# Halving the last network's inputs token by token and turning them by transposing transfers over DRAM instead of on TensorE, from the third group on

## The chip, the cores and the metric

The kernel runs on one core of one Trainium2 chip. The metric is the device time of one execution in microseconds, given as the median of several runs. Engines are named as the profile names them: PE (TensorE matmuls) and PEld (its weight loads), ACT (ScalarE), DVE (VectorE), POOL (GpSimd) and SP (SyncE), which issues most of the DMA transfers, in the order of its queue.

## The reference

Three stages over 3072 tokens of width 384. First a gated linear attention: per batch (4), head (8) and channel (48) a complex decay, a running state of 48 x 48, and an output y = q S. Then a mixture of 8 experts with a noisy gate: each token goes to its two best experts, and the results are summed with the gate's weights. Then the network that the change touches:

```
x = sum of the token's two expert rows, weighted        # 3072 x 384
h = maximum(maximum(x @ w1, x @ w2), x @ w3)            # 3072 x 768
out = h @ w_out                                         # 3072 x 384
```

## The kernel before

All operands of the large products are split into two f16 halves, a high and a low one, and each product is made as three f16 products (high x high, high x low, low x high) summed in PSUM.

Attention, gate and experts run first, in an order worked out by a planner written into the kernel (class `Order`). Behind them comes the last network, in program order, with the instructions of each engine put into that engine's queue by a list scheduler of the framework: what is ready first goes first, and among ready instructions the earlier in the program. It is this last part alone that the change touches.

The 24 blocks of 128 tokens are processed in seven groups, numbered here from 0: groups 0 and 1 have 2 blocks (256 tokens), groups 2 to 6 have 4 (512 tokens). Each group passes through four functions:

- `combine(g)` (L1508): for each of the group's blocks POOL gathers the two expert rows of every token from DRAM (tile `yg`, L1515, four buffers for each of the two), ACT scales the first (`za`, L1519, two buffers), DVE adds the scaled second (`z`, L1521). The blocks have tokens on the partitions.
- `turn(g)` (L1525): PE transposes each 128 x 128 piece of `z` into PSUM (`tz`, L1532, one buffer), three strips `k` of 128 channels, with the blocks of the group side by side; ACT writes the high half `zh` (L1533) and DVE the low half `zl` (L1534). Channels are then on the partitions.
- `hidden(g)` (L1537): for each of six strips `f` of the hidden width, PE makes three products u1, u2, u3 (L1553, 9 matmuls each: per `k` the pairs high-high, high-low, low-high), each into a PSUM tile `u` of five buffers. ACT copies the first (`mx`, L1561), DVE takes the maximum with the second (L1565) and third (L1566), ACT writes the high half `th` (L1567) and DVE the low half `tl` (L1568). The three PSUM tiles of a strip come free by L1561, L1565 and L1566.
- `last(g)` (L1570): for each block 18 matmuls (L1579) into `o` (two PSUM buffers), an ACT copy (L1582, three buffers), and a write of 192 KB by SP (L1585).

They are interleaved so:

```
combine(1)
for g in range(NG):
    hidden(g, range(0 if g else NPRE, KU), g + 1 if g + 1 < NG else None)
    last(g)
```

Within `hidden(g)` the next group is prepared. `turn(g + 1)` is issued behind the last matmul of the fifth strip (`f == KU - 2`), so its transposes stand on PE between matmuls near the end of `hidden(g)`. `combine(g + 1)`, for g of 1 to 5, is issued behind the first strip's ACT copy, so its ACT instructions stand behind that copy. Group 0 is gathered and turned earlier, by the planner.

The experts' part uses a transposing transfer already: `load_rows` (L1004) issues `dma_start_transpose` on SP, which reads 384 or 432 rows of 128 f16 values from the DRAM tensor `xs_rows` and puts them into `xa` with channels on the partitions. There are 96 of these.

Of the kernel before, what the change touches and what calls it, by code (L numbers as in the profile page):

```python
# [10 lines left out]
F16 = mybir.dt.float16  # L11
I32 = mybir.dt.int32
U32 = mybir.dt.uint32
AF = mybir.ActivationFunctionType
OP = mybir.AluOpType
# [17 lines left out]
    bufs=dict(bk=5, vg=2, wst=4, w1=1, w2=1, xa=2, hh=1, ya=2, ar=1, ai=1, iv=2, tn=1, r=1, ri=1, cs=3, fa=3,  # L33
           lam0=2, lam=6, lx=2, q=2, k=2, v=4, qr=3, kr=1, qc=2, kc=2, qt=2, kt=2, pm=2, xt=1, xhl=8, zp=1, fr=1,
           fh=4, car=1, sc=1, py=1, ps=1, lr=1, rw=3, w1b=1, w2b=1, raw=2, ua=1, vh=4, ch=1, cl=1),
# [213 lines left out]
def tile_kernel(ctx, tc, q, k, v, a_re, a_im, w_gate, w_noise, noise, w1, w2,  # L249
                u1, u2, u3, w_out, out):  # L250
    nc = tc.nc
    B, H, S, D = q.shape
    T = 128
    NC = S // T
    NI = B * NC
    NT = B * S
    HD = H * D
# [5 lines left out]
    KD = HD // 128  # L263
# [11 lines left out]

    FIRST = RA
    yf = nc.dram_tensor("yf_rows", (E * FIRST, HD), F32).ap()

    const = ctx.enter_context(tc.tile_pool(name="const", bufs=1, side="left"))
    EN = dict(POOL=nc.gpsimd, DVE=nc.vector)  # L280
# [80 lines left out]
    zl = const.tile([128, NI, 2 * E], F32, name="zl")  # L361
# [979 lines left out]
    GT = 512  # L1341
    GS = [2, 2] + [GT // T] * ((NT - GT) // GT)
# [4 lines left out]
    Z, TH = {}, {}  # L1347
# [65 lines left out]
    i = 0  # L1413
# [93 lines left out]
    def combine(g):  # L1507
        z = []  # L1508
        for t in range(GS[g]):
            i = sum(GS[:g]) + t  # L1510
            yy = []
            for s in range(2):
                y = fp.tile([128, HD], F32, name=f"yg{s}", bufs=4)
                src, row = (yf, sf) if (i + 1) * T <= FIRST else (ys, sy)
                nc.gpsimd.indirect_dma_start(out=y, out_offset=None, in_=src,  # L1515
                                             in_offset=bass.IndirectOffsetOnAxis(ap=row[:, i, s:s + 1], axis=0))
                yy.append(y)
            a = fp.tile([128, HD], F32, name="za", bufs=2)
            nc.scalar.activation(a, yy[0], AF.Copy, scale=wt[:, i, 0:1])  # L1519
            zt = fp.tile([128, HD], F32, name="z", bufs=TG + 1)  # L1520
            nc.vector.scalar_tensor_tensor(zt, yy[1], wt[:, i, 1:2], a, op0=OP.mult, op1=OP.add)  # L1521
            z.append(zt)
        Z[g] = z

    def turn(g):  # L1525
        z = Z[g]
        n = GS[g] * T
        zh, zl_ = (fp.tile([128, KD, GT], F16, name=x) for x in ("zh", "zl"))
        for k in range(KD):
            p = ptz.tile([128, GT], F32, name="tz")  # L1530
            for t in range(GS[g]):
                nc.tensor.transpose(p[:, t * T:(t + 1) * T], z[t][:, k * 128:(k + 1) * 128], ident)  # L1532
            nc.scalar.activation(zh[:, k, :n], p[:, :n], AF.Copy)  # L1533
            nc.vector.tensor_tensor(zl_[:, k, :n], p[:, :n], zh[:, k, :n], op=OP.subtract)  # L1534
        Z[g] = zh, zl_

    def hidden(g, fs_, then=None):  # L1537
# [6 lines left out]
        for f in fs_:  # L1544
            fs = slice(f * 128, (f + 1) * 128)
            ps = []
            for nm in ("u1", "u2", "u3"):
                uh, ul = U[nm]
                p = pu.tile([128, GT], F32, name="u")
                m = 0  # L1550
                for k in range(KD):
                    for w, x in ((uh, zh), (uh, zl_), (ul, zh)):
                        ins = nc.tensor.matmul(p[:, :n], w[:, k, fs], x[:, k, :n], start=(m == 0),  # L1553
                                               stop=(m == 3 * KD - 1))
                        m += 1
                ps.append(p[:, :n])
            if f == KU - 2 and then is not None:
                with tc.issue_after(ins.ins):
                    turn(then)
            a = fp.tile([128, GT], F32, name="mx", bufs=3)[:, :n]  # L1560
            ins = nc.scalar.activation(a, ps[0], AF.Copy)  # L1561
            if not f and 0 < g < NG - 1:
                with tc.issue_after(ins.ins):
                    combine(g + 1)
            nc.vector.tensor_tensor(a, a, ps[1], op=OP.max)  # L1565
            nc.vector.tensor_tensor(a, a, ps[2], op=OP.max)  # L1566
            nc.scalar.activation(th[:, f, :n], a, AF.Copy)  # L1567
            nc.vector.tensor_tensor(tl[:, f, :n], a, th[:, f, :n], op=OP.subtract)  # L1568
# [18 lines left out]
    fp = ctx.enter_context(tc.tile_pool(name="f", bufs=2, side="left"))  # L1587
# [3 lines left out]
    beyond()  # L1591
    po = ctx.enter_context(tc.tile_pool(name="po", bufs=2, space=PSUM))
# [3 lines that stand above are left out]
# [32 lines left out]
```

## Time and profile before

| | |
|---|---|
| median of 3 runs | 977.07 us (976.3 to 977.68) |
| the profiled execution | 977.96 us, span of its instructions 975.9 us |
| PE busy | 928.4 us (95% of the span) |
| DVE, ACT, POOL busy | 597.2 us (61%), 482.3 us (49%), 144.0 us (15%) |
| the last network's part | from about 677 us to the end |
| of the chain that ended last | PE 72%, DVE 11%, DMA 6%, ACT 6% |

The page of the profile gives busy times by engine, the same in 40 slices of the span (24.4 us each), and the chain of work that ended last: followed back from the last instruction, at each step to what released it or to the instruction before it on its engine. An engine's idle time costs something only where that chain passes through it. A line of the chain or of the timeline that merges several instructions gives their count behind an x.

### The profile page before, as it was taken

What the parts mean: (1) busy time and instruction counts of PE and PEld (TensorE: products, weight loads), DVE (VectorE), ACT (ScalarE), POOL (GpSimd) and SP (SyncE); (2) the same over time, 40 slices, a digit from 0 to 9 for tenths busy, and PEclk for the clock granted to TensorE, in tenths of its full rate; (3) what the DMA queues carried; (4) which work ended last, traced back from release to release, by engine and by line L of the source; (5) the groups of instructions that cost most, each with busy time, mean ns of one, the idle gap of its engine ahead of it and who ended that gap; (6) DMA issues with size and microseconds to landing.
All of it is one profiled execution on the core that took longest, in us unless ns stands there. A gap on an engine that the chain in (4) does not pass through costs nothing.

```text
span 975.9 us, 17033 instructions
## 1 busy us (share of the span) xinstructions
PE 928.4 (95%) x6372; PEld 587.5 (60%) x6372; DVE 597.2 (61%) x1407; ACT 482.3 (49%) x930; POOL 144.0 (15%) x201
## 2 busy tenths in 40 slices
PE   3989898999999999997989999998999999999998
PEld 1868787876666667653545555554784545454544
DVE  5988889996556658668988774542343232324231
ACT  7999889977444646523354444331232222322221
POOL 0102375231010004300010000000433030300000
PEclk9999998999999999998999999999999999999999
DMA  9999996995666565697658786631322020200000
GB/s 151 201 216 274 189 228 166 186 219 161 173 191 179 170 201 150 205 297 210 193 175 243 218 217 163 189 114 45 89 82 74 25 73 25 74 25 9 25 9 33
DMA packets 228636, 143.09 MB, mean 147 GB/s; under 512 B 179784, under 2 KB 216264, under 8 KB 228552
## 3 DMA queue, kind: packets, MB, share of 16 engines
q1 hardware_dynamic: 222408, 123.11, 49.3%
q0 software_dynamic: 6144, 18.88, 6.5%
q8 instruction: 50, 0.82, 0.4%
q14 instruction: 34, 0.28, 0.1%
HBM read 89.78 MB, written 41.88 MB: 135 GB/s over the span
## 4 chain that ended last, share of the span: by engine, by line
PE 72%; DVE 11%; DMA 6%; ACT 6%; issue 3%; SPq 1%; POOL 0%; ACTq 0%; POOLq 0%; DVEq 0%
PE u L1553 21%; PE bk L1035 8%; PE bk L1055 8%; PE o L1579 7%; PE bk L1096 7%; PE bk L1122 6%; PE sc L730 3%; DMA wst<-in_moe_w_dram 2%; PE bk L719 2%; PE ps L769 2%; PE py L748 2%; DMA raw<-in_moe_w_dram 1%; PE bk L552 1%; PE py L751 1%; PE bk L633 1%
## 5 line engine op out<-in xcount | busy, mean ns | idle before, releaser
L1055 PE MATMUL bk<-w,hh 128*128 128x384 f16 x576 | 99.2, 332 | 7.0 <-DVE w L985 5.8
L435 ACT ACTIVATE hh<-bk 128x384 f16<-128x384 f32 (+1 forms) x128 | 64.3, 508 | 79.7 <-PE bk L1096 42.4
L1035 PE MATMUL bk<-xa,w 128*128 128x384 f16 x576 | 99.0, 326 | 0.6 <-DMA xa<-xs_rows 0.6
L983 ACT ACTIVATE w<-wst 128x768 f16<-128x768 f32 (+1 forms) x77 | 71.4, 933 | 55.6 <-DMA wst<-in_moe_w_dram 24.0
L985 DVE SCALAR_TENSOR_TENSOR w<-wst,w 128x768 f16<-128x768 f32 (+1 forms) x77 | 81.0, 1066 | 11.7 <-ACT w L983 11.0
L1055 PEld LDWEIGHTS <-hh 128*128 128x128 f16 x576 | 56.6, 99 | 46.0 <-issue 10.1
L1122 PEld LDWEIGHTS <-hh 128*128 128x128 f16 x576 | 55.0, 98 | 39.8 <-issue 4.6
L1035 PEld LDWEIGHTS <-w 128*128 128x128 f16 x576 | 55.4, 98 | 36.1 <-issue 2.4
L1567 ACT ACTIVATE th<-mx 128x512 f16<-128x512 f32 (+1 forms) x42 | 23.8, 568 | 107.2 <-DVE mx L1566 107.2
L441 DVE COPY ya<-bk 128x384 f32<-128x384 f32 x30 | 16.7, 557 | 76.5 <-PE bk L1055 45.5
L938 POOL DMA_INDIRECT xs_rows<-xhl,sl x48 | 58.9, 1227 | 31.0 <-issue 10.1
L1565 DVE TENSOR_TENSOR mx<-mx,u 128x512 f32<-128x512 f32 (+1 forms) x42 | 25.6, 609 | 59.2 <-PE u L1553 59.1
L1515 POOL DMA_INDIRECT yg<-ys_rows,sy x42 | 42.8, 1020 | 120.7 <-ACT za L1519 105.1
L730 PE MATMUL sc<-qt,kt 96*128 96x128 f32 x384 | 53.5, 283 | 2.2 <-DVE pm L734 0.7
L1096 PE MATMUL bk<-xa,w1b 128*128 128x432 f16 x288 | 53.4, 346 | 1.8 <-DVE hh L1105 1.8
L1096 PE MATMUL bk<-xa,w 128*128 128x432 f16 x288 | 53.2, 346 | 0.0
L730 PEld LDWEIGHTS sc<-qt,kt 96*128 96x128 f32 x384 | 48.2, 194 | 6.4 <-issue 1.9
L1105 DVE SCALAR_TENSOR_TENSOR hh<-bk,hh 128x432 f16<-128x432 f32 x64 | 37.8, 603 | 17.0 <-ACT hh L435 16.8
L1122 PE MATMUL bk<-w2b,hh 128*128 128x384 f16 x288 | 48.2, 326 | 0.0
L1122 PE MATMUL bk<-w,hh 128*128 128x384 f16 x288 | 48.2, 326 | 0.0
L1521 DVE SCALAR_TENSOR_TENSOR z<-yg,wt,za 128x384 f32<-128x384 f32 x22 | 12.7, 614 | 56.6 <-ACT za L1519 52.0
L1579 PE MATMUL o<-woh,th 128*128 128x384 f16 x144 | 46.9, 326 | 0.0
(243 smaller groups left out, 2032.6 us busy)
## 6 DMA issues: line engine op xcount, KB each, us to landing
wst<-in_moe_w_dram SPq DMA_DIRECT2D x45, 512.0 KB
wst<-in_moe_w_dram SPq DMA_DIRECT2D x60, 384.0 KB
xs_rows<-wst SPq DMA_DIRECT2D x8, 1152.0 KB
ys_rows<-ya SPq DMA_DIRECT2D x48, 192.0 KB
raw<-in_moe_w_dram SPq DMA_DIRECT2D x9, 768.0 KB
ar<-in_a_re_dram SPq DMA_DIRECT2D x24, 192.0 KB
ai<-in_a_im_dram SPq DMA_DIRECT2D x24, 192.0 KB
q<-in_q_dram SPq DMA_DIRECT2D x24, 192.0 KB
```

The lines of the kernel that those rows point to most:

```text
L435: nc.scalar.activation(o, i, f, **kw)
L730: nc.tensor.matmul(tl("sc", (i, g))[:, j, :], tl("kt", i)[:, h, :], tl("qt", i)[:, h, :], start=True, stop=True)
L938: ins = nc.gpsimd.indirect_dma_start(out=xs, out_offset=bass.IndirectOffsetOnAxis(ap=sl[:, i, t:t + 1], axis=0), in_=tl("xhl", i), in_offs ...
L983: nc.scalar.activation(hi, src, AF.Copy, scale=scale)
L985: nc.vector.scalar_tensor_tensor(lo, src, scale, hi, op0=OP.mult, op1=OP.subtract)
L1035: nc.tensor.matmul(tl(*b)[:, :RA], tl("w1", e)[:, w, k, f * 128:(f + 1) * 128], tl("xa", e)[:, x + k, :RA], start=(k == m == 0), stop=(k = ...
L1055: nc.tensor.matmul(tl(*b)[:, :HD], tl("hh", e)[:, a, f, t * 128:(t + 1) * 128], tl("w2", e)[:, w, f], start=(f == m == 0), stop=(f == KF - ...
L1096: nc.tensor.matmul(tl(*b)[:, :RB], tl(n1, inst)[:, w, k, f * 128:(f + 1) * 128], tl("xa", xi)[:, x + k], start=(k == m == 0), stop=(k == K ...
L1122: nc.tensor.matmul(tl(*b)[:, :HD], tl("hh", xi)[:, a, f, ts_], tl(n2, inst)[:, w, f], start=(f == m == 0), stop=(f == KF - 1 and m == 2))
L1515: nc.gpsimd.indirect_dma_start(out=y, out_offset=None, in_=src, in_offset=bass.IndirectOffsetOnAxis(ap=row[:, i, s:s + 1], axis=0))
L1553: ins = nc.tensor.matmul(p[:, :n], w[:, k, fs], x[:, k, :n], start=(m == 0), stop=(m == 3 * KD - 1))
L1579: nc.tensor.matmul(p, a[:, f, ts_], w[:, f], start=(m == 0), stop=(m == 3 * KU - 1))
```

## The change

From group 2 on, `combine` does the halving, and `turn` returns at once. For each block, ACT copies `z` to f16 as the high half and DVE subtracts it to make the low half, both into one tile `zr` (128 tokens x 2 x 384 f16, three buffers), and SP writes the tile to a new DRAM tensor `z_rows`. Once the group's blocks are written, six transposing transfers on SP read 512 rows x 128 columns each and fill the three strips of `zh` and then the three of `zl`. Groups 0 and 1 stay as they were.

```diff
+    zs = nc.dram_tensor("z_rows", (NT, 2 * HD), F16).ap()
...
             zt = fp.tile([128, HD], F32, name="z", bufs=TG + 1)
             nc.vector.scalar_tensor_tensor(zt, yy[1], wt[:, i, 1:2], a, op0=OP.mult, op1=OP.add)
             z.append(zt)
+            if g > 1:
+                zr = fp.tile([128, 2, HD], F16, name="zr", bufs=3)
+                nc.scalar.activation(zr[:, 0], zt, AF.Copy)
+                nc.vector.tensor_tensor(zr[:, 1], zt, zr[:, 0], op=OP.subtract)
+                nc.sync.dma_start(zs[i * T:(i + 1) * T].rearrange("t (z d) -> t z d", z=2), zr)
         Z[g] = z
+        if g > 1:
+            r, n = sum(GS[:g]) * T, GS[g] * T
+            Z[g] = tuple(fp.tile([128, KD, GT], F16, name=x) for x in ("zh", "zl"))
+            for j in range(2 * KD):
+                nc.sync.dma_start_transpose(Z[g][j // KD][:, j % KD, :n], zs[r:r + n, j * 128:(j + 1) * 128])
 
     def turn(g):
+        if g > 1:
+            return
         z = Z[g]
```

## Rows read from the trace of the kernel before

**Rows 1.** The page's second part: TensorE's granted clock in 40 slices, tenths of full.
```profile
PEclk9999998999999999998999999999999999999999
```

**Rows 2.** Stretches of groups 1 and 2: length, busy by engine (count), clock, DMA share, GB/s.
```profile
707.60:732.80 25.20, 25.20 (x211) 20.50 (x210) 11.33 (x25) 9.48 (x21) 7.96 (x8) 1.00 0.26 80
732.80:781.05 48.25, 48.25 (x248) 24.16 (x246) 16.31 (x25) 13.05 (x23) 8.26 (x8) 1.00 0.16 50
```

**Rows 3.** The chain in order of time, groups 1, 2 and 6: start, us, what.
```profile
707.56 14.74 PE u L1553 x135
722.30 0.44 PE tz L1532 x4
...
724.16 0.65 PE tz L1532 x4
...
732.83 29.14 PE u L1553 x135
761.97 0.44 PE tz L1532 x4
...
763.92 0.56 PE tz L1532 x4
...
769.35 11.70 PE o L1579 x72
...
925.70 34.97 PE u L1553 x162
```

**Rows 4.** Line L1532, all transposes: min/median/max ns, first and last start, shape.
```profile
L1532 PE MATMUL tz<-ident,z x66: 272/273/329, 697.6 to 910.9; 128*128 128x128 f32 x66
```

**Rows 5.** Groups by shape from 676 us on: busy us, mean ns; idle and releaser.
```profile
L1568 DVE TENSOR_TENSOR tl<-mx,th 128x512 f16<-128x512 f32 x30 | 20.7, 691 | 18.1 <-ACT th L1567 18.1
L1567 ACT ACTIVATE th<-mx 128x512 f16<-128x512 f32 x30 | 18.9, 628 | 90.2 <-DVE mx L1566 90.2
L1534 DVE TENSOR_TENSOR zl<-tz,zh 128x512 f16<-128x512 f32 x15 | 10.4, 691 | 11.9 <-ACT zh L1533 11.8
L1533 ACT ACTIVATE zh<-tz 128x512 f16<-128x512 f32 x15 | 9.0, 597 | 26.4 <-PE tz L1532 26.4
L1568 DVE TENSOR_TENSOR tl<-mx,th 128x256 f16<-128x256 f32 x12 | 5.1, 423 | 4.3 <-ACT th L1567 4.3
```

**Rows 6.** Timeline of ACT, then DVE, around the combine of group 2.
```profile
708.92 1.11 ACT L1519 ACTIVATE za<-yg,wt 128x384 f32<-128x384 f32 x2
...
711.53 0.39 ACT L1561 ACTIVATE mx<-u 128x256 f32<-128x256 f32 x1 [0.17 <-PE u L1553]
...
710.96 1.14 DVE L1521 SCALAR_TENSOR_TENSOR z<-yg,wt,za 128x384 f32<-128x384 f32 x2
712.02 0.41 DVE L1566 TENSOR_TENSOR mx<-mx,u 128x256 f32<-128x256 f32 x1
```

**Rows 7.** Timeline of SP: transposing transfers of 384 rows, and groups 0 and 1's output writes.
```profile
196.66 1.13 SPq L1004 DMA_TRANSPOSE xa<-xs_rows  x1
...
215.81 6.30 SPq L1004 DMA_TRANSPOSE xa<-xs_rows  x5
...
705.19 28.53 SPq L1585 DMA_DIRECT2D out_dram<-o  x4
```

**Rows 8.** Timeline of PE: a matmul that waited for such a transfer.
```profile
201.86 0.97 PE L1035 MATMUL bk<-xa,w 128*128 128x384 f16 x5 [0.56 <-DMA xa<-xs_rows]
```

**Rows 9.** Stretches (columns as in rows 2): behind five transfers, after a stall, an output write.
```profile
222.00:223.00 1.00, 1.00 (x9) 0.61 (x7) 1.00 (x5) 1.00 (x4) 0.00 (x0) 1.00 0.43 98
223.00:224.00 1.00, 1.00 (x8) 0.61 (x7) 0.99 (x3) 0.96 (x4) 0.22 (x1) 1.00 0.00 0
683.50:686.70 3.20, 3.20 (x16) 2.27 (x17) 1.25 (x3) 0.42 (x1) 2.32 (x3) 0.50 0.23 66
706.00:707.00 1.00, 1.00 (x8) 0.61 (x7) 0.00 (x0) 0.00 (x0) 0.00 (x0) 1.00 0.53 197
```

**Rows 10.** Timeline of PE: the stall ahead of that stretch.
```profile
683.50 0.39 PE L1553 MATMUL u<-ua,u3l 128*128 128x256 f16 x1 [3.48 <-issue]
```

## The prediction

> **What bounds the kernel now.** The change touches the last network alone, so I first read which engine the end hangs on there. The chain in order of time [rows 3] shows, from 683 us to the last output block, nothing but PE pieces: products of the hidden layer (u), output products (o), and between them short pieces of transposes (tz). The stretches of groups 1 and 2 say the same from the other side: PE is busy for the whole length of each, 25.20 of 25.20 us and 48.25 of 48.25, while DVE is busy 16.31, ACT 13.05 and POOL 8.26 us of the 48.25 and the DMA engines 0.16 of it [rows 2]. The clock granted there is 1.00 of full, that is its upper level of 2.4 GHz [rows 1, 2]. So PE work taken out of these groups comes off the end, and work put on ACT, DVE and SP costs nothing while it is done before PE asks for its result or for the PSUM tiles that ACT and DVE drain.
>
> **What goes.** The transposes of groups 2 to 6, 60 of the 66 [rows 4]. One lasts 273 ns by itself, but they are pipelined, and what counts is their share of the chain. Group 2's stand in group 1's hidden part: 0.44 + 0.65 + 0.65 = 1.74 us. Group 3's stand in group 2's: 0.44 + 0.56 + 0.56 = 1.56 us; the pieces of 0.65 and 0.56 stand twice each, and groups 4 to 6 repeat group 3's pattern [rows 3]. Sum: 1.74 + 4 x 1.56 = 7.98 us. The waits for the single tz buffer lie inside these pieces. The check against a group that has no transposes in it: group 6's 162 hidden matmuls take 34.97 us, group 2's part lasts 769.35 - 732.83 = 36.52 us, a difference of 1.55 [rows 3]. I take 7.9 us, with 7.8 to 8.0 as its bounds.
>
> Per group ACT loses three `zh` copies (3 x 0.60) and DVE three `zl` subtractions (3 x 0.69) [rows 5].
>
> **What comes on ACT and DVE.** Per group four `zr` copies of 384 columns on ACT, each no more than the 0.63 us of a 512-column copy from SBUF, and four subtractions on DVE between 0.42 (256 columns) and 0.69 (512), so about 0.55 [rows 5]. That is 2.5 against 1.8 us before on ACT and 2.2 against 2.1 on DVE: the totals hardly move. What does move is their place: they now sit at the first strip of the hidden part, beside the work that frees PSUM tiles. Five `u` tiles rotate and a strip uses three, so a tile is asked for again five products later. In a group of 512 a product takes 9 x 29.14/135 = 1.94 us. The last combine of group 2 shows the tightest place, group 1 with 256 tokens, where a product takes 9 x 14.74/135 = 0.98 us [rows 3]: the tile that DVE frees at 712.43 (first strip's third product) is asked for at 707.56 + 7 x 0.98 = 714.4, and the tile that ACT frees at 711.92 (second strip's first) at 707.56 + 8 x 0.98 = 715.4 [rows 3, 6]. Margins: 2.0 and 3.5 us. If all four subtractions stand ahead of the first of these, 2.2 us are added and PE waits 0.2 us. There is also one new wait: `zr` has three buffers, so the fourth copy waits for the first write to land. In ACT's queue the rest of the strips' copies stand behind it. The first copy can start when the first `z` is there, two operations of some 0.6 us after 708.92 [rows 6], about 710.2, its subtraction ends near 711.4, and a write's bytes were all moved within 706 to 707 us after an issue at 705.19, 1.8 us [rows 7, 9]; so the fourth copy starts no later than about 713.9 with a little queueing, and a subtraction queued behind it ends by 715.2. The worst order would make PE wait some 1.5 us here, the best nothing. I take nothing, since DVE and ACT are filled by readiness and the maximum (L1566) already slips in as soon as its product is there. For groups of 512 the same margins are twice as long, 4 us and more, and cover it.
>
> **What comes on SP and the DMA engines.** Per group four writes of 192 KB and six transposing transfers. SP issues five transfers back to back in 6.30 us, 1.26 each, and a single one in 1.13 [rows 7]; the issue is what limits them, since in the last full microsecond of those five the DMA engines are busy 0.43 of the time at 98 GB/s, and from 223.00 on they move nothing, 0.9 us after the last issue ended at 222.11 [rows 9]. That 0.9 us is the lower bound of issue end to landing. The upper one is the matmul that waited for its transfer until 201.86: if it was the one issued at 196.66, 5.2 us from its start and 4.1 from its end [rows 7, 8]. The new transfers have 512 rows instead of 384; as no row shows them, I bound one by 1.13 to 1.68 us (1.26 x 512/384), and take 1.26, as the issue was what took the time.
>
> **When they are due.** Group 2 first. Its last `z` is ready at 712.10 [rows 6], the last `zr` between 713.4 and 715.5. The write takes 1.8 us, in the worst case as long as the slow transfer, 5.2. Six transfers last 6.8 to 10.1 us, and the last lands 0.9 to 4.1 us later. Earliest: 713.4 + 1.8 + 6.8 + 0.9 = 722.9. With the middle values 714.5 + 1.8 + 7.6 + 2.5 = 726.4. All four worst: 715.5 + 5.2 + 10.1 + 4.1 = 734.9. PE would come to group 2's hidden part at 732.83 - 1.74 = 731.1; its second matmul needs the fourth transfer, and the eighth, 1.5 us later, the sixth. So the sixth is due at 732.6: 6 us of margin in the middle, 2.3 us short in the worst corner. Beyond the margin a microsecond late costs a microsecond. For groups 3 to 6 the combine ends likewise some 7 us after the start of a hidden part of 36.5 us, with 11.70 us of output products behind it [rows 3]: at least 20 us of margin.
>
> Nothing else waits on SP in that time. Its four output writes of groups 0 and 1 stand between 705.19 and 733.72 [rows 7], two at the start and two at the end, and SP is otherwise idle there.
>
> **The sum.** The profiled execution took 977.96 us, span 975.9. Minus 7.9 that is 970.06. The median of the runs is 0.89 lower, 977.07, and gives 969.2 us, which I predict.
>
> **The rivals.** (a) A small price at group 1 and 2: the worst orders above, 0.2 to 1.5 us of PSUM waits and up to 2.3 us of late input, and slow matmuls behind a wait: after a stall of 3.48 us PE ran at a granted clock of 0.50, its lower level of 1.2 GHz, for 3.2 us and lost 1.6 us by it [rows 9, 10]. Together 0.5 to 5.4 us, time 969.7 to 974.6. For it: the margin of 2.0 us; against it: ready work goes first.
>
> (b) The transfers don't overlap each other, so that each takes the 5.2 us from issue to landing. Then six take 31.2 us. Groups 3 to 6 make it: group 3's could start some 10 us behind 732.83 and is due 48 us behind it. Group 2 doesn't: 714.5 + 1.8 + 31.2 = 747.5 against 732.6, 14.9 us late plus the 1.6 us of slow clock: 969.2 + 16.5 = 985.7, slower. It decides from about 3.8 us per transfer on (716.3 + 6 x 3.8 = 739.1, 6.5 late, which with the 1.6 eats the gain). Against it: five in 6.30 us with the engines empty 0.9 us later [rows 7, 9]. The Trainium skill, page "VectorE: DVE Perf Modes", section "The three transpose paths", speaks for it: it gives a 128x128 bf16 transpose 390 ns on TensorE and 1309 ns through the DMA crossbar, and its rules prefer TensorE when the result may go to PSUM. By that price, added up, a group's 24 pieces would take an estimated 31.4 us, and the time would be that of this rival; the trace disagrees, as five transfers of three pieces each were through in 7.2 us, 0.48 us a piece.
>
> (c) SP's queue is the new bound: the transfers of group g + 1 stand behind the output writes of group g, whose last is issued only after PE's last output product. Then each group's first two products wait about 1.0 + 6 x 1.26 + 0.9, some 9 us, and 1.6 us for the clock, five times: about 1020 us. Against it: the writes and transfers are earlier in the program and ready some 20 us earlier.
>
> (d) No gain: PE waits somewhere else for as much as it saves. The chain shows no second path within 8 us, so this is only a coincidence of (a) and (b).
>
> **Chances.** All hidden, 968.4 to 970.4: 0.70. (a): 0.14. (d): 0.05. (b): 0.06. (c) and other orders that starve PE: 0.05. What a measurement can tell from no change is 0.2%, 2 us: faster (below 975.1) 0.84, same 0.05, slower 0.11. The range takes in the forecast and (a), 967.8 to 974.6.
>
> **What would show it.** Right: no tz piece in the chain after 705 us but group 1's; hidden parts of 17.7 us (162 x 14.74/135) for group 1 and 35.0 for groups 2 to 5; PE without gaps; six transfers of 1.1 to 1.7 us on SP ending before 728 and then once per group. The forecast is wrong if PE's first matmul of a group waits for `zh` or `zl` (late input), or PE waits for `mx` at the second or third strip (PSUM), or if the transfers on SP stand behind the output writes.

## The result, and the profile after

The changed kernel took 968.5 us (median of 6 runs, 967.16 to 971.24), the one before 977.11 us beside it (6 runs): a ratio of 0.9908, 95% interval 0.9883 to 0.9932, so 6.6 to 11.4 us less. The forecast was 969.2 us, 7.9 us less, in a range of 967.8 to 974.6. Its profiled execution took 968.75 us, span 966.9.

The chain of waits of the kernel after, in order of time (start, us, what), answers to [rows 3]:
```profile
699.40 0.39 PE tz L1546 x2
...
706.62 17.68 PE u L1567 x162
724.31 5.85 PE o L1593 x36
730.16 34.96 PE u L1567 x162
765.12 11.70 PE o L1593 x72
776.82 34.97 PE u L1567 x162
...
963.57 0.49 ACT o L1596
```
The hidden part of group 2 was 29.14 us of matmuls, then three pieces of transposes between smaller ones; now it is one piece of 162 matmuls in 34.96 us, and group 1's is 17.68. No tz piece is left behind group 1's, at 700 us. The profile's list of waits has one line for PE behind 676 us, the stall at group 0 that stood there before as well [rows 10], and none for `zh`, `zl` or `mx`:
```profile
PE u L1567 <- issue: 3.5, 1, 3.5
```
From group 1's first matmul to the last copy of the output, the time was 972.45 - 707.56 = 264.89 us before and is 963.57 - 706.62 = 256.95 us after: 7.94 us less, against the 7.9 of the forecast.

The same stretches as in [rows 2], one group each (length, busy by engine, clock, DMA share, GB/s):
```profile
706.60:730.20 23.60, 23.60 (x200) 19.34 (x198) 11.29 (x26) 9.33 (x23) 8.64 (x8) 1.00 0.61 152
730.20:776.80 46.60, 46.60 (x235) 22.92 (x234) 16.31 (x26) 13.10 (x24) 8.44 (x8) 1.00 0.30 85
```
PE fills both from end to end. DVE (11.29 and 16.31 us, before 11.33 and 16.31) and ACT (9.33 and 13.10, before 9.48 and 13.05) are as busy as they were; what grew is the DMA share, 0.26 to 0.61 and 0.16 to 0.30. The clock stays at 1.00, its upper level of 2.4 GHz.

The new operations, grouped by shape (busy us, mean ns, idle before):
```profile
L1528 DVE TENSOR_TENSOR zr<-z,zr 128x384 f16<-128x384 f32 x20 | 10.8, 555 | 0.0
L1527 ACT ACTIVATE zr<-z 128x384 f16<-128x384 f32 x20 | 10.3, 515 | 4.4 <-DVE z L1523 3.5 <-DMA z_rows<-zr 0.9
```

### The profile page after: what moved, and what is told of

Read it like the earlier page. It is cut to its first block, busy times and chain, and to the rows that moved or that the text cites. A ratio compares the mean times of both kernels' runs of the same rounds, so it can differ in the third digit from the quotient of the medians.

```text
span 966.9 us, 17029 instructions
## 1 busy us (share of the span) xinstructions
PE 920.8 (95%) x6312; PEld 582.0 (60%) x6312; DVE 596.9 (62%) x1412; ACT 482.6 (50%) x935; POOL 144.4 (15%) x201
## 4 chain that ended last, share of the span: by engine, by line
PE 75%; DVE 11%; ACT 5%; DMA 4%; issue 3%; POOL 0%; SPq 0%; ACTq 0%; POOLq 0%; DVEq 0%
PE u L1567 22%; PE bk L1098 8%; PE bk L1037 8%; PE bk L1057 8%; PE bk L1124 7%; PE o L1593 7%; PE sc L732 3%; PE bk L721 2%; PE ps L771 2%; PE py L750 2%; PE bk L554 1%; PE bk L1131 1%; DMA wst<-in_moe_w_dram 1%; PE bk L635 1%; PE py L753 1%
## 5 line engine op out<-in xcount | busy, mean ns | idle before, releaser
L1579 DVE TENSOR_TENSOR mx<-mx,u 128x512 f32<-128x512 f32 (+1 forms) x42 | 25.6, 610 | 61.9 <-PE u L1567 61.8
L940 POOL DMA_INDIRECT xs_rows<-xhl,sl x48 | 58.2, 1212 | 31.4 <-issue 9.2
L1580 DVE TENSOR_TENSOR mx<-mx,u 128x512 f32<-128x512 f32 (+1 forms) x42 | 25.6, 610 | 36.0 <-PE u L1567 35.6
```

The lines of the kernel that those rows point to most:

```text
L940: ins = nc.gpsimd.indirect_dma_start(out=xs, out_offset=bass.IndirectOffsetOnAxis(ap=sl[:, i, t:t + 1], axis=0), in_=tl("xhl", i), in_offs ...
```

## The experiments

The chip that ran the first four was slower for every kernel: the kernel before took 1008.23 us there (21 runs). So they are compared by ratio, and by the trace from a group's first matmul on, where PE kept the same pace on both chips (162 hidden matmuls in 34.96 us).

**Both ways of turning at once.**
```diff
-            Z[g] = tuple(fp.tile([128, KD, GT], F16, name=x) for x in ("zh", "zl"))
+            X = tuple(fp.tile([128, KD, GT], F16, name=x, bufs=1) for x in ("xh", "xl"))
             for j in range(2 * KD):
-                nc.sync.dma_start_transpose(Z[g][j // KD][:, j % KD, :n], zs[r:r + n, j * 128:(j + 1) * 128])
+                nc.sync.dma_start_transpose(X[j // KD][:, j % KD, :n], zs[r:r + n, j * 128:(j + 1) * 128])
...
 def turn(g):
-        if g > 1:
-            return
```


> TensorE's transposes stay as before, and the whole added work runs beside them: the copies and subtractions to zr, the writes, and the six transposing transfers of each group, into two spare tiles that nobody reads. Theory 1 (the gain is the 60 transposes taken off TensorE, 7.9 us, and all that was added is covered): same as before, 977 +- 1 us, tz pieces of 1.5 to 1.7 us per group in the chain. Theory 2 (the added work costs TensorE something and the removal is worth more than 7.9): 1 us or more slower than before. Theory 3 (part of the gain, about 1 us, comes from a shift ahead of the last network): 976 us or less.

1008.3 us, ratio 0.9985 (0.9957 to 1.0013): no difference. Its chain has the tz pieces of [rows 3] again:
```profile
762.58 29.14 PE u L1565 x135
791.72 0.44 PE tz L1544 x4
...
793.67 0.56 PE tz L1544 x4
...
1002.21 0.49 ACT o L1594
```
From group 2's first matmul to the last copy it is 1002.21 - 762.58 = 239.63 us, in the kernel before 972.45 - 732.83 = 239.62. All that the change adds costs nothing there, with the transposes still on PE. Ahead of it, group 1 took 762.58 - 736.67 = 25.91 us in this trace, in the kernel before 25.27. Of the 0.64 us more, 0.5 are a wait of PE's transposes for a `zl` subtraction on DVE, and DVE had stood idle until 749.63, 5 us after its last `zr` operation. What held it up the trace doesn't show; the doubled transfers below have the same copies and subtractions in group 1 and no such delay (23.7 us, without transposes).

**Neither way.**
```diff
 def combine(g):
-            if g > 1:
-                zr = fp.tile([128, 2, HD], F16, name="zr", bufs=3)
...
-                nc.sync.dma_start(zs[i * T:(i + 1) * T].rearrange("t (z d) -> t z d", z=2), zr)
-        if g > 1:
...
-                nc.sync.dma_start_transpose(Z[g][j // KD][:, j % KD, :n], zs[r:r + n, j * 128:(j + 1) * 128])
+        if g == 2:
+            Z["x"] = tuple(fp.tile([128, KD, GT], F16, name=x, bufs=1) for x in ("xh", "xl"))
+            for x in Z["x"]:
+                nc.gpsimd.memset(x, 0.5)
 def turn(g):
         if g > 1:
+            Z[g] = Z["x"]
             return
```


> Neither way of turning: no transposes on TensorE from group 2 on, no halving to zr, no write, no transposing transfer; groups 2 to 6 read two constant tiles instead of their inputs, so their output is not the reference's. This is the floor of what the change can give. Theory 1: equal to the changed kernel, 968.5 to 969.2 us. Theory 2: 1 us or more below the changed kernel, 967 us or less. Theory 3: as theory 1 from the hidden part on, with TensorE reaching group 1 as early as in the changed kernel.

1001.23 us, ratio 0.9937 (0.9913 to 0.9961), its interval overlapping that of the changed kernel.
```profile
759.94 34.96 PE u L1562 x162
...
993.35 0.49 ACT o L1591
```
From group 2 on 993.35 - 759.94 = 233.41 us; the changed kernel has 963.57 - 730.16 = 233.41. There the changed kernel stands on the floor. Ahead of that, group 1, this kernel can't tell: on this chip PE lost 1.0 us in two waits for nothing that the profile shows, which the traces of the kernels before and after don't have.

**Each transfer twice.** Before each useful transposing transfer one into a spare tile.
```diff
+            X = tuple(fp.tile([128, KD, GT], F16, name=x, bufs=1) for x in ("xh", "xl"))
             for j in range(2 * KD):
+                nc.sync.dma_start_transpose(X[j // KD][:, j % KD, :n], zs[r:r + n, j * 128:(j + 1) * 128])
                 nc.sync.dma_start_transpose(Z[g][j // KD][:, j % KD, :n], zs[r:r + n, j * 128:(j + 1) * 128])
```


> Each transposing transfer is preceded by an equal one into a spare tile, 12 per group. By the margins of theory 1: SP begins the twelve of group 2 at about 718.6 us, at 1.26 us each the eighth is issued by 728.7 and the twelfth by 733.7, and lands 1 to 2 us later; TensorE wants group 2 at 730.2 and the last half 1.5 us later. So group 2 is 3 to 4 us late, with up to 1.6 us more for the lower clock behind the wait; groups 3 to 6 keep more than 10 us of margin: 971.5 to 974.5 us, one wait of TensorE in the whole tail. Rival (the transfers are limited by the DMA engines, not by their issue): longer than 1.3 us each, group 2 later by 10 us and more, 979 us or more. Rival (more margin than worked out): no change, 968.5 us.

1004.82 us, ratio 0.9973 (0.995 to 0.9997), 3.6 us above the kernel with neither by the medians. SP's timeline around group 2, and PE's two waits there:
```profile
753.09 1.26 SPq L1537 DMA_TRANSPOSE zh<-z_rows  x1
...
764.29 1.26 SPq L1537 DMA_TRANSPOSE zl<-z_rows  x1
765.59 1.26 SPq L1536 DMA_TRANSPOSE xl<-z_rows  x1
766.89 1.26 SPq L1537 DMA_TRANSPOSE zl<-z_rows  x1
```
```profile
767.03 0.38 PE L1569 MATMUL u<-zl,u1h 128*128 128x512 f16 x1 [1.75 <-DMA zl<-z_rows]
...
767.47 0.38 PE L1569 MATMUL u<-zh,u1h 128*128 128x512 f16 x1
769.71 0.59 PE L1569 MATMUL u<-zl,u1h 128*128 128x512 f16 x1 [1.86 <-DMA zl<-z_rows]
```
Twice as many transfers still follow each other at 1.26 us, so the rival with longer ones falls. The doubling alone doesn't tell whether the issue or the DMA engines set that pace; that 384 rows took the same 1.26 us [rows 7], with the DMA engines 0.43 busy [rows 9], speaks for the issue. PE now waits for the last `zl` strips, twice, 3.6 us in all, and only at group 2: the groups behind it follow each other in 46.66 us as in the changed kernel. The price is more than the waits: from group 1's first matmul to the last copy it is 1003.11 - 740.45 = 262.66 us, 5.71 more than in the changed kernel and inside the 3 to 6 expected, as PE ran at a lower granted clock behind the second wait (0.75 over these 5 us):
```profile
770.00:775.00 5.00, 5.00 (x19) 2.06 (x18) 2.53 (x5) 3.55 (x7) 2.21 (x3) 0.75 0.21 65
```
The trace also measures the landing: the last transfer's issue ends at 768.15, PE goes on at 769.71, 1.6 us later.

**The transfers behind the output writes.** The six transfers move into a function `fetch`, issued on SP behind the last output write of the group before.
```diff
 def last(g):
-            nc.sync.dma_start(out[r:r + T], o)
+            W = nc.sync.dma_start(out[r:r + T], o)
+        with tc.issue_after(W.ins):
+            fetch(g + 1)
```


> The six transposing transfers of each group are issued on SP behind the last output write of the group before, in place of some 20 us earlier: the cover is taken away, five times. Theory 1: each group's first products wait for four transfers and their landing, about 5 to 7 us behind the last output write's issue, which itself is about 1 us behind TensorE's last output product, then for two more, and a part of it runs at the lower clock: 8 to 11 us per group, 1010 to 1025 us. Rival (the transfers are covered anyway, for instance by products that TensorE still has): below 985 us.

1037.84 us, ratio 1.0288 (1.0263 to 1.0314), 36.6 us above the kernel with neither by the medians, less than the 41 to 56 expected (1010 to 1025 against 969). The chain from group 2 to group 4, shortened:
```profile
765.14 36.84 PE u L1569 x157
801.98 11.71 PE o L1595 x72
813.77 0.50 ACT o L1598
...
814.79 1.12 SPq L1537
...
818.56 2.65 DMA zl<-z_rows
821.26 36.15 PE u L1569 x157
...
876.75 35.67 PE u L1569 x157
```
From group 2 to group 3 it is 821.26 - 765.14 = 56.12 us instead of 46.66, 9.5 us more, and then 876.75 - 821.26 = 55.49, 8.8 more (the next two 8.4 and 8.5): the lower half of the 8 to 11 expected. From group 1's first matmul to the last copy this execution took 1035.59 - 733.89 = 301.70 us, 44.75 more than the changed kernel, inside the 41 to 56. It was the slowest of its four, and why the medians lie only 36.6 apart isn't shown; the kernel's runs differ by 4 us here, those of the kernel with neither by 6. The chain leaves PE and goes through the output copy, SP and the landing. Behind the wait PE runs at a granted 0.50, the lower clock of 1.2 GHz, for a while:
```profile
765.00:770.00 5.00, 4.86 (x12) 1.74 (x12) 0.06 (x1) 1.19 (x3) 0.00 (x0) 0.50 0.23 52
```
So the price of a transfer is there; only its place in SP's queue hides it.

**The changed kernel again, and group 1 turned by transfers too.** In the second, `g > 1` becomes `g > 0` in its three places. Both ran on one chip, the kernel before taking 977.04 us there (11 runs).

> The changed kernel as it is, once more, timed beside the next one on one chip. All theories: 0.989 to 0.994 of the kernel before; theory 1 wants it equal to the kernel that has neither way of turning (0.9937 of the kernel before), within 0.003.

> Group 1 is halved and turned by transfers too, which takes another 0.22 + 0.39 + 0.39 = 1.0 us of transposes off the chain. Theory 1: the second block's z is ready at about 687 to 689, its write lands by 693 even beside the gathers, six transfers of 1.13 to 1.26 us end at 700.5 and land by 702; TensorE comes to group 1 at about 705.6: covered, 1.0 us less than the changed kernel (0.999 of it), no tz piece left but those of group 0. Rival (the gathers of group 2, which run beside it, hold up the transfers): TensorE waits for zh or zl at the start of group 1, 0 to 4 us slower than the changed kernel.

969.13 us, ratio 0.9912 (0.9889 to 0.9935), for the changed kernel, 7.9 us less than before, with 966.10 - 709.15 = 256.95 us from group 1 on as in its first trace; 967.54 us, ratio 0.9914 (0.989 to 0.9938), with group 1. The measurement can't tell them apart. The trace shows what was to be had: no tz piece is left, and group 1 is not late.
```profile
683.54 15.68 PE u L1567 x142
...
705.07 17.68 PE u L1567 x162
```
From group 1 on it has 962.01 - 705.07 = 256.94 us, as the changed kernel's 256.95. The 1.0 us of tz pieces ahead of that (0.22 and twice 0.39) is gone from the chain. That this version gains that much is shown by the chain alone, not by the times.

**No gathers beside the writes.**
```diff
-            for s in range(2):
+            for s in range(2 if g < 3 else 0):
...
+            if g == 2:
+                TH["y", t] = yy
+            if g > 2:
+                yy = TH["y", t]
```


> Groups 3 to 6 gather nothing and combine the rows that group 2 gathered, so their output is not the reference's. In the changed kernel SP goes from the issue of a group's fourth write to its first transposing transfer in 3.95, 4.53, 4.38 and 4.41 us for groups 2 to 5, beside which the gathers of the next group run, and in 1.54 us for group 6, beside which none run. If the gathers hold up the landing of the writes, all five take 1.5 to 1.8 us here. If it is something else that sets group 6 apart, groups 2 to 5 keep 4 us and more. The time is that of the changed kernel either way, as the lag is covered.

SP's timeline, the changed kernel first (groups 2, 3 and 6), then this one (groups 2, 3 and 6):
```profile
710.60 4.04 SPq L1529 DMA_DIRECT2D z_rows<-zr  x4
718.59 3.81 SPq L1535 DMA_TRANSPOSE zh<-z_rows  x3
722.44 4.86 SPq L1535 DMA_TRANSPOSE zl<-z_rows  x3
...
735.57 4.32 SPq L1529 DMA_DIRECT2D z_rows<-zr  x4
744.42 3.73 SPq L1535 DMA_TRANSPOSE zh<-z_rows  x3
...
875.50 4.32 SPq L1529 DMA_DIRECT2D z_rows<-zr  x4
881.36 3.73 SPq L1535 DMA_TRANSPOSE zh<-z_rows  x3
```
```profile
713.09 3.98 SPq L1533 DMA_DIRECT2D z_rows<-zr  x4
718.78 3.77 SPq L1539 DMA_TRANSPOSE zh<-z_rows  x3
...
738.06 4.32 SPq L1533 DMA_DIRECT2D z_rows<-zr  x4
744.00 4.71 SPq L1539 DMA_TRANSPOSE zh<-z_rows  x3
...
878.00 4.32 SPq L1533 DMA_DIRECT2D z_rows<-zr  x4
883.85 3.73 SPq L1539 DMA_TRANSPOSE zh<-z_rows  x3
```
From the end of the fourth write's issue to the first transfer it is 3.95, 4.53 and 1.54 us in the changed kernel and 1.71, 1.62 and 1.53 us without the gathers (groups 4 and 5: 4.38 and 4.41 against 1.63 and 1.68). The gathers of the next group hold up the writes by 2.2 to 2.9 us. The time, 971.24 us in one run, shows no gain from their absence, as expected of a lag that is covered.

## Why the prediction was right

**What bounds.** That PE alone sets the end in this part was the step on which everything rests, and the two kernels with both and with neither way of turning show it from both sides: 239.63 us from group 2 on with the transposes and all the added work, 233.41 with neither, 239.62 before and 233.41 after. Of the 7.94 us that the trace lost from group 1 on, 6.21 lie there; the other 1.73 are group 1's, whose part shrank from 25.27 to 23.54 us, as predicted for the transposes of group 2 (1.74). The two profiled spans differ by 9.0 us, and the remaining 1.1 lie almost all ahead of group 1. There PE came to its long wait at group 0 earlier, and was past it at 681.50 instead of 683.50, but another run of the same changed kernel was past it at 684.96. So that start moves by more than 1.1 us between runs of one kernel, and nothing is left for theory 3, a gain from a shift ahead of the last network. The medians agree: 8.6 us less beside the first run, 7.9 beside the second.

**ACT and DVE.** A copy took 515 ns (no more than 628 was assumed) and a subtraction 555 (0.55). Group 1 was the tightest place, as predicted:
```profile
712.48 0.41 DVE L1580 TENSOR_TENSOR mx<-mx,u 128x256 f32<-128x256 f32 x1
713.67 0.61 DVE L1528 TENSOR_TENSOR zr<-z,zr 128x384 f16<-128x384 f32 x1
712.83 0.52 ACT L1527 ACTIVATE zr<-z 128x384 f16<-128x384 f32 x1 [0.93 <-DMA z_rows<-zr]
```
The maximum with the third product, L1580, ended at 712.89 where PE asked for its tile at 706.62 + 7 x 0.98 = 713.5, a margin of 0.6 us instead of 2.0. Three of the four subtractions stood ahead of it. The reason given for taking nothing, that the maximum slips in as soon as its product is there, didn't hold: the product was made by 706.62 + 3 x 0.98 = 709.6 and the maximum began at 712.48, and in the kernel before it began 1.5 us after its product too [rows 3, 6]. So taking nothing came out right by a margin of 0.6 us, and not for the reason given. The fourth copy did wait for the first write to land, 0.9 us, and the strips' copies behind it were in time. Rival (a) came that near and no nearer.

**SP and the transfers.** 1.25 to 1.26 us each for 512 rows, against 1.26 taken, and so the 384 rows of [rows 7] cost as much to issue. The bound of 1.68 was too low: one of the 30 took 2.25, and of the kernel before's own 96, of 384 and 432 rows, one took 5.91 (median 1.13).
```profile
L1535 SPq DMA_TRANSPOSE zl<-z_rows x15: 1258/1261/2249, 722.4 to 887.7; - x15
```
Rival (b), 5.2 us each, is refuted by these times and by the doubled transfers. With it falls the sum that the prediction made of a price in the Trainium skill, page "VectorE: DVE Perf Modes", section "The three transpose paths": 1309 ns for each 128x128 piece, an estimated 31.4 us a group. Group 2's 24 pieces were issued in 8.7 us here (718.59 to 727.30), 0.36 a piece. Rival (c) had its price somewhat high, 10.6 us a group where 8.4 to 9.5 were measured, and its condition wrong: SP's queue holds the transfers ahead of the output writes.

**The term that was mis-sized** is the landing of the writes before the transfers: 1.8 us was taken from an output write with nothing beside it [rows 9], and 4.3 us passed from the last `zr` (714.28) to the first transfer of group 2 (718.59), inside the bound of 5.2 but far from the value taken; the runs without gathers show why (3.95 us of it behind the last write's issue, against 1.71). With one of the six slowed to 2.25 us (the three of `zl` took 4.86 us together, above) the last was issued by 727.30 and, with 1.6 us of landing, there at about 728.9 (an estimate with the landing of the doubled transfers). PE asked for it at 730.16 + 1.51 = 731.7. The margin at group 2 was thus 2.8 us, not the 6 of the middle values. The doubled transfers, with six more of 1.26, used it up as they should.

## What to carry to other kernels

Where the chain shows one engine without a gap, the price of an operation is its share of that engine's chain (0.11 to 0.16 us for a transpose here, not its 273 ns), and another path for it that is ten times longer (some 17 us from group 2's last z at 712.09 to the landing, where its transposes took 1.74) costs nothing as long as it ends before its due time: work out that time for the tightest group, not the average one. Look then at where the new instructions stand in their queue, since the same six transfers cost nothing ahead of the output writes and 8.4 to 9.5 us a group behind them. Take a transfer's landing from a row with the same neighbours on the DMA engines, not from a quiet stretch.

## What the runs showed of the hardware that was not expected

Gathers beside them more than double the time from the issue of a group's last 192 KB write until all its writes have landed: 3.95 to 4.53 us against 1.53 to 1.71. By the profile the DMA engines are not full meanwhile, though their share is a rough measure (it reads 1.43 between 723 and 724 us); in the microsecond in which group 2's last write was issued they were 0.77 busy at 187 GB/s:
```profile
714.00:715.00 1.00, 1.00 (x12) 0.90 (x10) 0.98 (x4) 0.47 (x2) 0.69 (x2) 1.00 0.77 187
```
And the same wait doesn't always have the same clock behind it. Behind the stall of 3.4 to 3.5 us at group 0, PE ran at a granted 0.50, the lower level, for 3.2 us in the kernel before [rows 9], and for 3 us and part of the next 3 in the changed one, but at 1.00 in the version with group 1, with as long a wait:
```profile
681.50:684.50 3.00, 3.00 (x15) 2.08 (x16) 1.22 (x3) 0.42 (x1) 2.10 (x3) 0.50 0.23 66
684.50:687.50 3.00, 3.00 (x19) 2.20 (x18) 1.08 (x3) 0.89 (x2) 2.39 (x3) 0.61 0.58 146
```
```profile
683.54:686.70 3.16, 3.16 (x29) 2.83 (x30) 1.80 (x4) 1.32 (x3) 2.20 (x3) 1.00 0.24 82
```
So the 1.6 us that the prediction put on the clock behind a wait is one outcome among several; what decides between them stays open.
